# Attention and gated product on one core: x of two batches summed in DRAM, one transpose for rows 0 and 2, normalisation spread over other engines

## The chip, the core and the metric

One core of a Trainium2 chip runs the whole program. The metric is the time of one launch in microseconds (us) on the device. Of the kernel before three runs were timed: 625.11, 625.5 and 626.14 us, median 625.5 us. One more execution was profiled; all rows below come from it.

## The reference

The inputs are q, k and v (4 batches, 12 heads, 448 positions, 64 wide) and three weight matrices. What is computed, cut to what matters:

```python
scores = (q @ k.transpose(0, 1, 3, 2)) / 8          # per batch and head, 448 x 448
scores = where(mask_above_diagonal, -1e9, scores)
attn = exp(scores - max(scores)); attn = attn / (sum(attn) + 1e-9)
x = (attn @ v).transpose(0, 2, 1, 3).reshape(1792, 768)
out = ((x @ w_a) * (x @ w_b)) @ w_out               # 768 -> 1536 -> 768
```

The weights arrive as 64-bit floats and are turned into 32-bit ones on the chip.

## The kernel before, in words

The work falls into three stretches. In the **front** (to about 90 us) attention runs for batches 0 and 1, as 12 head pairs, six of each batch. In the **middle** (to about 252 us) the twelve head pairs of batches 2 and 3, called late pairs here, are threaded between the products of batches 0 and 1. After that come only products: batches 2 and 3, and parts of batches 0 and 1 in a seven-product scheme.

One head pair of attention goes like this. `scores` multiplies q and k in 64x64 tiles of TensorE (PE), two heads side by side, one row block r of 64 query positions at a time (r = 0 to 6, with 64(r+1) columns, since the mask is causal). VectorE (DVE) takes the row minimum of the negated scores (L459), ScalarE (ACT) the exponential and its sum (L465), DVE the reciprocal of the sums (L472, L474). Then each row block is normalised (L475 to L484): by GpSimd (POOL) in the front, by ACT in late pairs. `turn` transposes the normalised rows, 128 columns at a time, 16 transposes a pair (L501), into the PSUM banks t0 and t1, which ACT or DVE copy to `pt` (L299, L291). `values` multiplies with v: in the front with 128x64 tiles (L521), in late pairs with four 64x64 tiles at once (L540), row half 0 into bank `pv` and row half 1 into a bank of the ring `m`; ACT copies one, DVE adds the other, the sum is `acc`.

A front pair's x is kept as two fp32r parts, `x_hi` and `x_lo`. Later `take` (L602) builds the seven-product operands for batches 0 and 1: twelve DVE additions x_hi + x_lo into `pt` tiles, then differences and splits.

A product (L684) is three matmuls of 448 columns (hi*hi, lo*hi, hi*lo). Weights are converted on DVE with five instructions a unit (L346 to L358) and split on ACT and DVE.

What sets the order: the kernel records every operation in a `Plan`. Its `order()` plays all engines forward with costs (`dve_ns`, `act_ns`, `pool_ns`, `WAIT`) and issues the instructions in that order, so each engine's queue is fixed when the program is built, and every engine takes its queue in turn. `SLACK` holds a late pair's transposes back by that many ns in the plan; `PACE` says behind which front pair a weight unit is converted; `TAKES` at which place `take` runs. Loads and stores go through SyncE's queue (SP); DMAs that add into DRAM (L315) are issued by GpSimd.

Of the kernel before, what the change touches and what calls it, by code (L numbers as in the profile page):

```python
# [18 lines left out]
P = 128  # L19
# [12 lines left out]
PW = PO[NR]  # L32
FIRST, SECOND = ((6,), (5, 0)), ((4, 1), (3, 2))
# [3 lines left out]
NORM = ("pool", "pool", "act", "act")  # L37
TAKE = (("act", "dve"), ("act", "dve"), ("act", "act"), ("act", "act"))
# [4 lines left out]
TAKES = (15, 16, 17)  # L43
# [4 lines left out]
PACE = (0, 0, 0, 0, 0, 0, 0, 0, 1, 0, 1, 0, 0)  # L48
# [17 lines left out]
SLACK = (0, 0, 600, 600)  # L66
# [22 lines left out]
class Plan:  # L89
# [42 lines left out]
    def order(self):  # L132
# [7 lines left out]
        dge = dma = 0.0  # L140
# [9 lines left out]
        while count < n:  # L150
# [34 lines left out]
            if e == "sp":  # L185
                free[e] = at + 60.0
                dge = max(dge, at + 700.0) + 630.0
                dma = max(dma, dge) + self.ops[i][1]
                end[i] = dma + 1150.0
            elif self.ops[i][5] == "d":  # L190
                free[e] = at + 1100.0
                end[i] = free[e] + self.ops[i][1]
# [39 lines left out]
def dma_ns(nbytes):  # L232
    return nbytes / 360.0
# [3 lines left out]
def causal_attention_then_gated_product(  # L237
# [45 lines left out]
    w_m = sbuf.tile([P, 2, UW], U32, tag="w_m", name="w_m")  # L283
    w_keep = [dram.tile([P, UW], F32, name=f"w_keep{u}") for u in range(NU)]
# [28 lines left out]
    def add_up(nbytes, o, i, reads, writes):  # L313
        plan.op("pool", nbytes / 150.0 + 2500.0,
# [18 lines left out]
    def convert_unit(besides=False):  # L333
# [9 lines left out]
        def r():  # L343
# [3 lines left out]
            out=e.t, in0=high(), scalar1=0x7FF00000, scalar2=None, op0=ALU.bitwise_and), [t], [e])  # L347
        plan.op("dve", 470, lambda: nc.vector.tensor_scalar(
            out=m.t, in0=high(), scalar1=0x000FFFFF, scalar2=0x00100000,
            op0=ALU.bitwise_and, op1=ALU.bitwise_or), [t], [m])  # L350
# [74 lines left out]
    def scores(b, hp):  # L425
# [7 lines left out]
        def view(r):  # L433
            return p.t[:, PO[r]:PO[r] + D * (r + 1)]

        for part, tags in ((FIRST, ("s0", "s1")), (SECOND, ("m", "m") if b < 2 else ("t0", "t1"))):
            banks = [bank(tag, 3 if tag == "m" else 1) for tag in tags]
# [17 lines left out]
            for r in [r for rs in part for r in rs]:  # L455
# [16 lines left out]
        plan.op("dve", 200, lambda: nc.vector.tensor_scalar_add(st.t[:, rc, 0:NR], st.t[:, sm, 0:NR], 1.0e-9),  # L472
                [(st, sm, r) for r in rows], [(st, rc, r) for r in rows])
        plan.op("dve", 122, lambda: nc.vector.reciprocal(st.t[:, rc, 0:NR], st.t[:, rc, 0:NR]), [], [(st, rc, r) for r in rows])  # L474
        for r in rows:  # L475
            def norm(r=r):
                if NORM[b] == "act":
# [4 lines left out]

            ns = act_ns(D * (r + 1), False, 1) if NORM[b] == "act" else pool_ns(D * (r + 1))
            plan.op(NORM[b], ns, norm, [(st, rc, r)], [(p, r)])  # L484
# [4 lines left out]
    def turn(b, hp, n):  # L489
        p = p_of[b, hp]  # L490
        full = sb("pt", 3, [P, 2, 8, D])
        places = [(c, r) for c, o, count in groups[n] for r in range(2 * c, NR)]
        for h in range(2):
            t = bank(f"t{h}")
            some = list(enumerate(places[4 * h:4 * h + 4]))
            for part in [[x] for x in some] if b < 2 else [some]:

                def mm(part=part, t=t):
                    for i, (c, r) in part:
                        at = PO[r] + P * c - (D if b >= 2 and c == 3 else 0)  # L500
                        x = nc.tensor.matmul(  # L501
                            t.t[:, P * i:P * (i + 1)], p.t[:, at:at + P],
                            swapped if r in CROSSED else ident, is_transpose=True, start=True, stop=True,
# [3 lines left out]
                plan.op("pe", 109 * len(part), mm, [*((p, r) for _, (_, r) in part), "ident"], [t], slack=SLACK[b])  # L507
            copy(TAKE[b][h], 512, lambda full=full, h=h: full.t[:, :, 4 * h:4 * h + 4, :],
                 lambda t=t: t.t.rearrange("p (i j d) -> p j i d", i=4, j=2), [t], [(full, h)], True)
        pt[n] = full  # L510

    def values(b, hp, x):
# [3 lines left out]
        if x is not None:  # L516
# [12 lines left out]
            split_x(x, hp, lambda: ps.t[:, :S], ps, True)  # L529
            return  # L530
        more = m_bank()

        def quarters():
            for k in (0, 1, 3, 2, 5, 4, 6):
                c, row = (3, 1) if k == 6 else divmod(k, 2)
                n, o = next((n, g[1]) for n in range(2) for g in groups[n] if g[0] == c)
                o += k - 2 * c
                rows = slice(row * D, (row + 1) * D)
                for j in range(2):
                    r = nc.tensor.matmul(  # L540
                        (ps, more)[row].t[j * D:(j + 1) * D, D * k:S], vt.t[rows, c, j, :],
                        parts[n].t[rows, j, o:o + NR - k, :].rearrange("p i d -> p (i d)"), start=k < 2, stop=k in (4, 6),
# [3 lines left out]
        plan.op("pe", 15 * 107.0, quarters,  # L546
                [(vt, 0), (vt, 1), *((parts[n], h) for n in range(2) for h in range(2))], [ps, more], "q")
# [53 lines left out]

    def take(k):  # L602
        rooms = [sb("pt", 3, [P, 1024]) for _ in range(2)]
        b11, b12, b21, b22 = (((lambda t=t, i=i: t.t[:, i * S:(i + 1) * S]), (t, i)) for t in rooms for i in range(2))
        for (o, key), b, kk in ((b11, 0, k), (b12, 1, k), (b22, 1, k + 3), (b21, 0, k + 3)):
            hi, lo = xs[b]
            both(o, lambda hi=hi, kk=kk: hi.t[:, kk, :].bitcast(F32), lambda lo=lo, kk=kk: lo.t[:, kk, :].bitcast(F32), ALU.add,
                 [(hi, kk), (lo, kk)], [key])
# [502 lines left out]
```

## Time and profile before

| | us |
|---|---|
| median of the three timed runs | 625.5 |
| the profiled execution, its own time | 625.17 |
| its span, first to last instruction | 623.4 |
| PE busy in the span | 614.5 |
| DVE, ACT, POOL busy | 554.5, 390.5, 64.8 |

What lies around the span is 625.17 - 623.4 = 1.8 us. "Busy" counts the time in which at least one instruction of an engine runs; matmuls overlap each other, so a PE matmul's own duration is longer than the spacing from one to the next. A wait is idle time of an engine, put down to what ended it.

### The profile page before, as it was taken

How to read it: one execution, taken by the hardware profiler on the slowest of the kernel's cores; microseconds unless marked ns; L12 is line 12 of the kernel's file. 1: busy time of each engine (PE TensorE's matmuls, PEld its weight loads, DVE VectorE, ACT ScalarE, POOL GpSimd, SP SyncE). 2: the span in 40 equal slices, each digit the busy share in tenths (PEclk: the TensorE clock that was granted, in tenths of full speed). 3: DMA queues.
4: the chain of work that ended last, by engine and by line, in shares of the span. 5: the costliest groups of instructions: out<-in, count | busy, mean ns of one | idle time of the engine just before them, and what ended most of it. 6: DMA issues, size and time to landing. Idle time of an engine off the chain costs nothing.

```text
span 623.4 us, 11323 instructions
## 1 busy us (share of the span) xinstructions
PE 614.5 (99%) x3980; PEld 543.8 (87%) x3980; DVE 554.5 (89%) x1243; ACT 390.5 (63%) x932; POOL 64.8 (10%) x124
## 2 busy tenths in 40 slices
PE   8999999999999999999999999999999999999997
PEld 6666778888888888899999999999999999999997
DVE  7789978999999999999989997588899767889984
ACT  6989549999999999455344655344455433455530
POOL 4756320000000000000000022100000000000030
PEclk9999999999999999999999999999999999999999
DMA  8636443987686769733311668412112532112454
GB/s 277 234 116 211 157 159 109 301 269 242 248 268 243 228 244 313 261 111 102 127 52 71 214 122 201 103 52 76 52 50 97 174 110 76 53 61 83 108 90 98
DMA packets 40568, 96.02 MB, mean 154 GB/s; under 512 B 4672, under 2 KB 25152, under 8 KB 40512
## 3 DMA queue, kind: packets, MB, share of 16 engines
q1 hardware_dynamic: 37632, 90.72, 43.6%
q0 software_dynamic: 2880, 4.59, 5.3%
q8 instruction: 31, 0.51, 0.3%
q14 instruction: 25, 0.20, 0.1%
HBM read 67.37 MB, written 27.92 MB: 153 GB/s over the span
## 4 chain that ended last, share of the span: by engine, by line
PE 90%; DVE 6%; DMA 2%; ACT 1%; POOL 0%; issue 0%; SPq 0%; DVEq 0%; POOLq 0%
PE m L684 63%; PE t L684 7%; PE t L501 5%; PE s L684 3%; PE s L450 3%; DMA raw<-kT 2%; PE pv L684 2%; PE t L450 2%; PE pv L540 2%; PE m L540 1%; PE pv L521 1%; ACT early L465 1%; DVE pt L299 1%; DVE p L459 1%; PE m L450 1%; DVE early L459 1%
## 5 line engine op out<-in xcount | busy, mean ns | idle before, releaser
L684 PE MATMUL m<-x_hi,w_hi 128*128 128x448 f32 x360 | 135.1, 375 | 0.0
L684 PE MATMUL m<-x_lo,w_hi 128*128 128x448 f32 x360 | 130.5, 362 | 0.0
L684 PE MATMUL m<-x_hi,w_lo 128*128 128x448 f32 x360 | 130.3, 362 | 0.0
L291 ACT ACTIVATE w_hi<-w 128x384 fp32r<-128x384 f32 (+1 forms) x96 | 57.5, 599 | 31.1 <-PE m L684 12.0
L684 PEld LDWEIGHTS m<-x_hi,w_hi 128*128 128x128 f32 x360 | 67.8, 188 | 5.2 <-issue 0.4
L684 PEld LDWEIGHTS m<-x_hi,w_lo 128*128 128x128 f32 x360 | 67.5, 187 | 4.8
L684 PEld LDWEIGHTS m<-x_lo,w_hi 128*128 128x128 f32 x360 | 67.7, 188 | 3.6
L315 POOL DMA_DIRECT2D out<-mid x20 | 17.7, 905 | 507.1 <-ACT mid L291 497.6
L291 ACT ACTIVATE mid<-m 128x448 f32<-128x448 f32 x72 | 38.8, 541 | 45.9 <-PE m L684 38.9
L465 ACT ACTIVATE p<-p,st 128x128 f32<-128x128 f32 (+6 forms) x126 | 62.3, 499 | 8.1 <-DVE st L459 8.0
L291 ACT ACTIVATE w_hi<-w_e_s 128x384 fp32r<-128x384 f32 x72 | 37.3, 521 | 45.8 <-PE m L684 25.0
L307 DVE TENSOR_TENSOR w_lo<-w,w_hi 128x384 fp32r<-128x384 f32 (+1 forms) x96 | 62.9, 655 | 0.9 <-ACT w_hi L291 0.9
L684 PE MATMUL m<-g_hi,w_hi 128*128 128x448 f32 x144 | 53.3, 370 | 1.2 <-DVE acc L307 1.2
L307 DVE TENSOR_TENSOR w_lo<-w_e_s,w_hi 128x384 fp32r<-128x384 f32 x72 | 39.6, 550 | 14.7 <-ACT w_hi L291 13.6
L684 PE MATMUL m<-g_lo,w_hi 128*128 128x448 f32 x144 | 52.3, 363 | 0.0
L684 PE MATMUL m<-g_hi,w_lo 128*128 128x448 f32 x144 | 52.1, 362 | 0.0
L291 ACT ACTIVATE pt<-t 128x512 f32<-128x512 f32 x72 | 41.9, 594 | 10.6 <-PE t L501 10.1
L684 PE MATMUL m<-p_x,w_hi 128*128 128x448 f32 x144 | 43.4, 362 | 0.0
L291 ACT ACTIVATE g_hi<-mid 128x448 fp32r<-128x448 f32 x42 | 24.2, 575 | 19.0 <-DVE mid L307 19.0
L478 ACT ACTIVATE p<-p,st 128x64 f32<-128x64 f32 (+6 forms) x84 | 34.9, 500 | 1.1 <-DVE st L474 0.9
L355 DVE SCALAR_TENSOR_TENSOR w_e<-w,w_e 128x768 uint32<-128x768 uint32 x36 | 34.6, 960 | 0.3 <-ACT w_e L351 0.2
L353 DVE SCALAR_TENSOR_TENSOR w_m<-w_m,w 128x768 f32<-128x768 uint32 x36 | 34.3, 952 | 0.2
(178 smaller groups left out, 1471.0 us busy)
## 6 DMA issues: line engine op xcount, KB each, us to landing
w<-w SPq DMA_DIRECT2D x36, 768.0 KB, 5.9
w<-w_keep SPq DMA_DIRECT2D x48, 384.0 KB, 3.0
w_keep<-w SPq DMA_DIRECT2D x36, 384.0 KB, 5.3
raw<-qT SPq DMA_DIRECT2D x24, 224.0 KB, 4.5
raw<-kT SPq DMA_DIRECT2D x24, 224.0 KB, 4.6
v<-v SPq DMA_DIRECT2D x24, 192.0 KB, 4.3
out<-mid SPq DMA_DIRECT2D x20, 224.0 KB, 2.4
out<-mid POOLq DMA_DIRECT2D x20, 224.0 KB, 3.9
```

The lines of the kernel that those rows point to most:

```text
L291: return nc.scalar.activation(o(), i(), AF.Copy)
L307: plan.op(engine, ns, lambda: e.tensor_tensor(out=o(), in0=a(), in1=b(), op=op), reads, writes)
L315: lambda: nc.gpsimd.dma_start(out=o(), in_=i(), accum_op=ALU.add), reads, writes, "d")
L353: plan.op("dve", 869, lambda: nc.vector.scalar_tensor_tensor(out=r(), in0=m.t, scalar=2.0**32, in1=low(), op0=ALU.mult, op1=ALU.add), [m, ...
L355: plan.op("dve", 869, lambda: nc.vector.scalar_tensor_tensor(out=e.t, in0=high(), scalar=0x80000000, in1=e.t, op0=ALU.bitwise_and, op1=ALU ...
L450: x = nc.tensor.matmul(at[r][0].t[to * D:(to + 1) * D, at[r][1]], q[:, r * D:(r + 1) * D], k[:, 0:D * (r + 1)], start=True, stop=True)
L459: return nc.vector.tensor_tensor_reduce(out=view(r), in0=at[r][0].t[:, at[r][1]], in1=mask[:, S - n:], scale=-0.125, scalar=3.0e38, op0=AL ...
L465: return nc.scalar.activation(view(r), view(r), AF.Exp, bias=st.t[:, nm, r:r + 1], scale=-1.0, accum_out=st.t[:, sm, r:r + 1],)
L478: return nc.scalar.activation(view(r), view(r), AF.Copy, scale=st.t[:, rc, r:r + 1])
L501: x = nc.tensor.matmul(t.t[:, P * i:P * (i + 1)], p.t[:, at:at + P], swapped if r in CROSSED else ident, is_transpose=True, start=True, st ...
L540: r = nc.tensor.matmul((ps, more)[row].t[j * D:(j + 1) * D, D * k:S], vt.t[rows, c, j, :], parts[n].t[rows, j, o:o + NR - k, :].rearrange( ...
L684: r = nc.tensor.matmul(ps.t[:, :S], a[:, i, :], x(), start=first and n == 0, stop=last and n == 2, skip_group_check=part)
```

## The change

- **x in DRAM.** After each front pair `keep_x` stores `x_hi` to DRAM (SP) and adds `x_lo` to it with an accumulating DMA (POOL). `take` loads the sums instead of adding on DVE, and `TAKES` is (13, 15, 16), not (15, 16, 17).
- **Late pairs, transposes.** The rows of p lie close together (`LATE_PO`), rows 0 and 2 share one 128-column transpose, 15 instead of 16 a pair. Row 0's own columns now come out in row half 1 of `pt`, so `values` needs the first 64 positions of v there: a small load a pair on SP puts them into the spare end of p (`LATE_V`). The eight 64x64 steps of `values` then have 896 columns in each row half, where before it was 960 and 832. ACT now copies the `m` bank, DVE adds `pv`.
- **Normalisation.** In late pairs GpSimd does rows 3 and 6, ACT the other five. The last two front pairs are normalised by ACT, not GpSimd. The first pair's rows go to DVE (0 to 2), GpSimd (3 to 5) and ACT (6), with the reciprocal in three steps.
- **Order.** Pair 1's scores are recorded right behind pair 0's, into other banks. `PACE` is one pair later. The planner's costs change: DMA rate 340 instead of 360, accumulating DMAs, a port that DVE's bit operations and GpSimd hold in turn, `SLACK` 400 instead of 600.

```diff
-TAKES = (15, 16, 17)
+TAKES = (13, 15, 16)
...
-SLACK = (0, 0, 600, 600)
+SLACK = (0, 0, 400, 400)
...
+                if e == "pool" or self.ops[i][5] == "x":
+                    at = max(at, port)
+                    port = at + ns
...
+        if b >= 2:
+            load(D * P * 4, lambda: p.t[D:, LATE_V:LATE_V + P].rearrange("p (j d) -> p j d", j=2), lambda: v0[b, hp, 0:D, 0],
+                 [], [(p, "v")])
...
+            by = NORM0[r] if (b, hp) < (0, 1) else "pool" if r in BY_POOL and b >= 2 else NORM[b] if (b, hp) < (1, NP - LATE) else "act"
...
+                halves = [((2, 0), two(2, 2)[1]), *(two(r, 2) for r in (3, 4, 5))], [two(6, 2), *(two(r, 4) for r in (4, 5, 6))]
...
+            for row, k, n, o, count in ((1, -1, 1, 0, 1), (0, 0, 0, 0, 6), (1, 1, 0, 0, 6), (0, 2, 1, 0, 5), (1, 3, 1, 1, 4),
+                                        (0, 4, 1, 5, 3), (1, 5, 1, 6, 2), (1, 6, 0, 6, 1)):
...
-        copy("act", S, lambda: t.t, lambda: ps.t[:, :S], [ps], [t], True)
-        two_input("dve", S - D, lambda: t.t[:, D:], lambda: more.t[:, D:S], lambda: t.t[:, D:], ALU.add, [more], [t])
+        copy("act", S, lambda: t.t, lambda: more.t[:, :S], [more], [t], True)
+        two_input("dve", S - D, lambda: t.t[:, D:], lambda: ps.t[:, D:S], lambda: t.t[:, D:], ALU.add, [ps], [t])
...
+    def keep_x(b, k):
+        hi, lo = xs[b]
+        load(P * S * 4, lambda: x_first[b][k], lambda: hi.t[:, k, :].bitcast(F32), [(hi, k)], [("x1", b, k)])
+        add_up(P * S * 4, lambda: x_first[b][k], lambda: lo.t[:, k, :].bitcast(F32), [(lo, k)], [("x1", b, k)])
...
-            both(o, lambda hi=hi, kk=kk: hi.t[:, kk, :].bitcast(F32), lambda lo=lo, kk=kk: lo.t[:, kk, :].bitcast(F32), ALU.add,
-                 [(hi, kk), (lo, kk)], [key])
+            load(P * S * 4, o, lambda b=b, kk=kk: x_first[b][kk], [("x1", b, kk)], [key])
...
-            scores(*pairs[i])
+            for n in {0: (0, 1), 1: ()}.get(i, (i,)):
+                scores(*pairs[n])
```

Three places in the built programs, on the engines of which the prediction speaks. Names carry the ring's buffer number and a running number.

PE, the values of the last late pair and the first product behind them, before (pv and m are the two PSUM banks, pt the transposed rows, v the values):

```order
L684 MATMUL m0_3246<-g_hi_1320,w_lo_79 128x448
L540 MATMUL pv0_3304<-pt1_3251,v2_74 64x448 x2
L540 MATMUL m1_3307<-pt1_3251,v2_74 64x384 x2
L540 MATMUL m1_3307<-pt2_3278,v2_74 64x256 x2
L540 MATMUL pv0_3304<-pt2_3278,v2_74 64x320 x2
L540 MATMUL m1_3307<-pt2_3278,v2_74 64x128 x2
L540 MATMUL pv0_3304<-pt2_3278,v2_74 64x192 x2
L540 MATMUL m1_3307<-pt1_3251,v2_74 64x64 x2
L684 MATMUL m1_3337<-g_hi_1320,w_hi_78 128x448
```

The same place now:

```order
L731 MATMUL m1_3287<-g_hi_1362,w_lo_79 128x448
L583 MATMUL m0_3334<-pt2_3309,p1_71 64x64 x2
L583 MATMUL pv0_3337<-pt1_3285,v2_74 64x384 x2
L583 MATMUL m0_3334<-pt1_3285,v2_74 64x384 x2
L583 MATMUL pv0_3337<-pt2_3309,v2_74 64x320 x2
L583 MATMUL m0_3334<-pt2_3309,v2_74 64x256 x2
L583 MATMUL pv0_3337<-pt2_3309,v2_74 64x192 x2
L583 MATMUL m0_3334<-pt2_3309,v2_74 64x128 x2
L583 MATMUL m0_3334<-pt1_3285,v2_74 64x64 x2
L731 MATMUL m2_3361<-g_hi_1362,w_hi_78 128x448
```

Before, the next product writes the bank m1 that values has just filled; now it writes m2, and six matmuls stand ahead of the first one into m0. The two banks' column counts are 960 and 832 before, 896 and 896 now.

PE in the front, from the end of pair 0's values to the scores of pair 4 (raw0), before (t00 and t10 are the transpose banks):

```order
L521 MATMUL pv0_405<-pt0_358,v0_72 64x64 x2
L501 MATMUL t10_421<-ident_66,p1_71 128x128
L501 MATMUL t10_421<-swapped_67,p1_71 128x128
L501 MATMUL t10_421<-ident_66,p1_71 128x128 x2
L501 MATMUL t00_433<-swapped_67,p1_71 128x128 x2
L501 MATMUL t00_433<-ident_66,p1_71 128x128
L501 MATMUL t00_433<-swapped_67,p1_71 128x128
L450 MATMUL s00_441<-raw0_239 64x448 x2
```

And now:

```order
L561 MATMUL pv0_410<-pt0_363,v0_72 64x64 x2
L539 MATMUL t00_400<-swapped_67,p1_71 128x128
L539 MATMUL t10_432<-ident_66,p1_71 128x128
L539 MATMUL t10_432<-swapped_67,p1_71 128x128
L539 MATMUL t10_432<-ident_66,p1_71 128x128 x2
L469 MATMUL s00_446<-raw0_260 64x448 x2
```

Before, 8 transposes of pair 1 stand here behind 4 that went ahead of the values; now 5 stand here behind 3. Four fewer are done when pair 4's scores come up.

GpSimd in the front now, around the first of the new accumulating DMAs (early holds p of pairs 2 and 3; these rows are pair 2's last two and pair 3's first four):

```order
L506 TENSOR_SCALAR early_75<-early_75,st_69 128x384
L506 TENSOR_SCALAR early_75<-early_75,st_69 128x448
L506 TENSOR_SCALAR early_75<-early_75,st_69 128x64
L506 TENSOR_SCALAR early_75<-early_75,st_69 128x128
L326 DMA x_first0_0_81<-x_lo0_457 128x448
L506 TENSOR_SCALAR early_75<-early_75,st_69 128x192
L506 TENSOR_SCALAR early_75<-early_75,st_69 128x256
```

Before, the seven rows of pair 3 stand there without a DMA between them. Twelve such DMAs now stand in this queue, the last five in a row behind pair 9, ahead of the first late pair's rows 3 and 6.

## Rows read from the trace of the kernel before

**Rows 1.** Page, part 1: busy us, share of the span and instructions by engine

```profile
PE 614.5 (99%) x3980; PEld 543.8 (87%) x3980; DVE 554.5 (89%) x1243; ACT 390.5 (63%) x932; POOL 64.8 (10%) x124
```

**Rows 2.** PE's waits, whole span: who, for whom, total us, times, longest

```profile
PE m L684 <- DVE acc L307: 1.2, 1, 1.2
...
PE t L501 <- DVE pt L299: 1.0, 2, 0.6
PE s L450 <- DMA raw<-kT: 0.8, 2, 0.5
PE t L501 <- ACT pt L291: 0.7, 1, 0.7
PE t L501 <- POOL early L479: 0.5, 2, 0.3
```

**Rows 3.** Chain of waits: start us, us, what; late transposes, then the front

```profile
128.06 0.44 PE t L501 x4
...
11.44 8.71 DMA raw<-kT
20.29 0.99 PE s L450 x8
...
26.13 0.92 PE s L450 x8
```

**Rows 4.** Timeline of PE, end of a late pair's values: start us, us, instruction, count

```profile
123.02 0.27 PE L540 MATMUL m<-pt,v 64*64 64x64 f32 x3
...
123.16 0.34 PE L540 MATMUL pv<-pt,v 64*64 64x192 f32 x2
```

**Rows 5.** Timeline, all engines, where the last late pair's values end

```profile
250.43 0.33 PE L540 MATMUL pv<-pt,v 64*64 64x192 f32 x2
250.81 0.54 ACT L291 ACTIVATE acc<-pv 128x448 f32<-128x448 f32 x1 [1.21 <-PE pv L540]
250.82 0.62 DVE L307 TENSOR_TENSOR pt<-x_hi,x_lo 128x448 f32<-128x448 f32 x1
...
251.38 0.56 DVE L307 TENSOR_TENSOR acc<-m,acc 128x384 f32<-128x384 f32 x1
...
252.00 0.47 PE L684 MATMUL m<-g_hi,w_hi 128*128 128x448 f32 x1 [1.24 <-DVE acc L307]
```

**Rows 6.** Busy us by engine in windows (count), clock, DMA share, GB/s

```profile
12.00:20.00 8.00, 7.41 (x70) 4.95 (x70) 5.97 (x29) 8.00 (x30) 6.49 (x15) 1.00 1.01 370
...
57.00:84.00 27.00, 25.62 (x192) 19.02 (x193) 23.37 (x60) 16.36 (x46) 12.99 (x21) 1.00 0.49 163
84.00:250.00 166.00, 166.00 (x1375) 143.62 (x1377) 160.16 (x377) 152.14 (x384) 0.24 (x1) 1.00 0.71 241
```

The columns after the window's length are PE, PEld, DVE, ACT, POOL.

**Rows 7.** Timeline, GpSimd's norms in the front and one DVE instruction beside them

```profile
21.38 0.66 POOL L479 TENSOR_SCALAR early<-early,st 128x448 f32<-128x448 f32 x1
...
54.69 1.30 DVE L307 TENSOR_TENSOR w_lo<-w,w_hi 128x768 fp32r<-128x768 f32 x1
...
55.15 1.34 POOL L479 TENSOR_SCALAR p<-p,st 128x448 f32<-128x448 f32 x1
...
79.66 4.59 POOL L479 TENSOR_SCALAR early<-early,st 128x64 f32<-128x64 f32 x7 [9.97 <-DVE st L474]
```

**Rows 8.** Timeline of one late pair: reciprocal, ACT's seven norms, first transpose

```profile
121.51 0.95 DVE L307 TENSOR_TENSOR w_lo<-w,w_hi 128x768 fp32r<-128x768 f32 x1
...
125.18 0.20 DVE L474 RECIPROCAL st<-st 128x7 f32<-128x7 f32 x1
...
125.42 2.91 ACT L478 ACTIVATE p<-p,st 128x64 f32<-128x64 f32 x7
...
127.90 0.27 PE L501 MATMUL t<-swapped,p 128*128 128x128 f32 x1
```

**Rows 9.** DVE's instructions on pt, 100 to 300 us: count, ns min/median/max, from, to

```profile
L307 DVE TENSOR_TENSOR pt<-x_hi,x_lo x12: 611/615/617, 249.4 to 267.3; 128x448 f32<-128x448 f32 x12
```

**Rows 10.** Page, part 5: busy us, mean ns of one, idle before

```profile
L315 POOL DMA_DIRECT2D out<-mid x20 | 17.7, 905 | 507.1 <-ACT mid L291 497.6
```

More of the change, by code (lines that the diff above doesn't have):

```diff
@@ L283, in causal_attention_then_gated_product @@
     w_m = sbuf.tile([P, 2, UW], U32, tag="w_m", name="w_m")
+    x_first = [[dram.tile([P, S], F32, name=f"x_first{b}_{k}") for k in range(KT)] for b in range(2)]
     w_keep = [dram.tile([P, UW], F32, name=f"w_keep{u}") for u in range(NU)]
@@ L491, in turn, with two @@
         full = sb("pt", 3, [P, 2, 8, D])
-        places = [(c, r) for c, o, count in groups[n] for r in range(2 * c, NR)]
+        if b < 2:
+            places = [((r,), p.t[:, PO[r] + P * c:PO[r] + P * (c + 1)]) for c, o, count in groups[n] for r in range(2 * c, NR)]
+            halves = places[:4], places[4:]
+        else:
+            def two(r, k):
+                return (r,), p.t[:, LATE_PO[r] + D * k:LATE_PO[r] + D * (k + 2)]
+            if n == 0:
+                halves = [two(r, 0) for r in (1, 2, 3, 4)], [two(5, 0), two(6, 0), two(6, 5)]
+            else:
+                halves = [((2, 0), two(2, 2)[1]), *(two(r, 2) for r in (3, 4, 5))], [two(6, 2), *(two(r, 4) for r in (4, 5, 6))]
@@ L493, in turn @@
+        at = 0
         for h in range(2):
             t = bank(f"t{h}")
-            some = list(enumerate(places[4 * h:4 * h + 4]))
+            some = list(enumerate(halves[h]))
             for part in [[x] for x in some] if b < 2 else [some]:
                 def mm(part=part, t=t):
-                    for i, (c, r) in part:
-                        at = PO[r] + P * c - (D if b >= 2 and c == 3 else 0)
+                    for i, (rs, of) in part:
                         x = nc.tensor.matmul(
-                            t.t[:, P * i:P * (i + 1)], p.t[:, at:at + P],
-                            swapped if r in CROSSED else ident, is_transpose=True, start=True, stop=True,
-                        )
-                    return x
-                plan.op("pe", 109 * len(part), mm, [*((p, r) for _, (_, r) in part), "ident"], [t], slack=SLACK[b])
@@ L508, in turn @@
-            copy(TAKE[b][h], 512, lambda full=full, h=h: full.t[:, :, 4 * h:4 * h + 4, :],
-                 lambda t=t: t.t.rearrange("p (i j d) -> p j i d", i=4, j=2), [t], [(full, h)], True)
+                            t.t[:, P * i:P * (i + 1)], of,
+                            swapped if rs[0] in CROSSED else ident, is_transpose=True, start=True, stop=True,
+                        )
+                    return x
+                plan.op("pe", 109 * len(part), mm, [*((p, r) for _, (rs, _) in part for r in rs), "ident"], [t], slack=SLACK[b])
@@ L510, in turn @@
+            count = len(some)
+            copy(TAKE[b][h], P * count, lambda full=full, at=at, count=count: full.t[:, :, at:at + count, :],
+                 lambda t=t, count=count: t.t[:, :P * count].rearrange("p (i j d) -> p j i d", i=count, j=2), [t], [(full, h)], True)
+            at += count
         pt[n] = full
```

72 lines of the change are left out of this document (45 added, 27 removed).

## The prediction

> **What bounds the kernel now.** I read the shares of the engines first: PE is busy for 614.5 of 623.4 us, DVE for 554.5 [rows 1]. So a change gains either by taking work off PE or by removing one of PE's few waits, and a relief of another engine is worth nothing unless PE waits for it. Then PE's waits over the whole span: the five listed add up to 4.2 us, and the longest single one is 1.24 us, where a product waits for DVE's addition of the last late pair [rows 2, 5]. Of the transposes' waits (1.0, 0.7 and 0.5 us) 0.6 us lies in the start-up and 1.6 us between 57 and 84 us. The windows say where these can lie at all: from 84 to 250 us PE is busy for 166.00 of 166 us, between 57 and 84 us for 25.62 of 27 [rows 6]. In the middle only less PE work helps; in the front a better fit may.
>
> **The change part by part.** The sum is made against the profiled execution's own 625.17 us; the median of the three runs is 0.3 us above it.
>
> *One transpose less a late pair.* Four transposes take 0.44 us on the chain, 0.11 us each [rows 3]. There are 12 late pairs: 12 x 0.11 = 1.32 us off PE. It is on the path, because PE has no idle time there. The bounds are close; I take 1.32.
>
> *Values with even halves.* The columns multiplied stay the same, 1792 for each head, but the halves become 896 and 896. In the trace the row half in bank m ends at 123.02 + 0.27 = 123.29 and the one in pv at 123.16 + 0.34 = 123.50 [rows 4]: 0.21 us late for 128 columns more. Evening them takes half of that, 0.105 us a pair, 1.26 us in all. The lower end is nothing, if the added pair of 64-column steps costs as much in issue as it saves; I take 1.26, since the step sizes in between stay as they were. The small load of v that it needs, one a late pair on SP, waits for a buffer that was freed two pairs earlier; behind it in the queue stand loads of later pairs, and PE waits for no DMA in the middle.
>
> *The bank behind the last values.* Before, the next product writes m1, which DVE has yet to read: values' last matmul begins at 250.43, ACT copies pv from 250.81, DVE is in an addition on pt until it adds m at 251.38, and PE goes on at 252.00 after 1.24 us idle [rows 5]. Now the m bank is read by ACT's copy, 0.54 us in the trace, and the next product writes another bank; six matmuls stand ahead of the one that needs the copied bank. Six matmuls are longer than one copy, so the wait goes: 1.24 us. What is late next there is nothing that the trace shows: PE has no further wait to the end [rows 2]. For the other late pairs the exchange of banks is worth nothing.
>
> *x through DRAM.* Twelve additions of 0.615 us leave DVE, between 249.4 and 267.3 us [rows 9], 7.4 us. I count them at nothing: PE does not wait there, except behind the bank above. If that cover were wrong they could be worth up to 7.4 us, but no wait of PE bears it out. What comes in: 12 stores and 12 loads on SP, and 12 accumulating DMAs at 0.905 us of GpSimd each [rows 10]. An accumulating DMA waits for the store of the same tile to land, and GpSimd's norms of later pairs are queued behind it; PE's transposes wait for those. A norm of a whole pair takes 4.59 us at its slowest [rows 7]; with 0.9 us of DMA that is 5.5, and PE's period in the front is 26.13 - 20.29 = 5.84 us [rows 3]. It fits, barely in the worst pairs. The last five DMAs stand in a row ahead of the first late pair's rows 3 and 6; 4.5 us of issue, in a stretch where GpSimd has nothing else to do. Cost taken: nothing. Bounds: nothing to 2.9 us, from the longest landing of a load in the front, 8.71 us, less the period of 5.84.
>
> *The first pair on three engines, pair 1's scores earlier.* These make pair 0's transposes ready sooner. But pair 4's scores begin at 20.29 us when kT lands, 8.71 us after its issue, with the DMA engines full (1.01, 370 GB/s) [rows 3, 6]. The bytes queued ahead of it are the same now, so that landing stays at about 20.2 us, and what is won before it is waited away again. In the new order four transposes fewer stand ahead of those scores, so PE has 4 x 0.11 = 0.44 us more left to do from there on. I take a loss of 0.44; the bounds are 0.44 lost and nothing.
>
> *The front's end.* Between 57 and 84 us PE waits 0.5 us for GpSimd's norms, and 1.1 us for copies out of the transpose banks [rows 2]. The slow one is the last pair's 4.59 us [rows 7]. In the change the last two pairs' norms are ACT's, 2.91 us for seven [rows 8], and ACT has 27 - 16.36 = 10.6 us free there [rows 6], so the 0.5 goes. The 11th and 12th pairs also come sooner, with the first weight unit one pair later, so copies and conversions meet elsewhere; half of the 1.1 us is a guess. I take 1.0 of the 1.6; bounds nothing and 1.6.
>
> *Rows 3 and 6 on GpSimd.* ACT loses some 10 us of 152.14 [rows 6], which frees nothing that PE waits for. What is added is a wait of PE on GpSimd. GpSimd and DVE hinder each other: a 448-wide norm takes 0.66 us, and 1.34 with DVE's w_lo beside it, which itself takes 1.30 and not 0.95 [rows 7, 8]. In a late pair the reciprocal ends at 125.38 and the first transpose is at 127.90, 2.5 us later [rows 8]. Row 6 is now the sixth of seven in a block, 0.55 us later still. Two clear norms need at most 2 x 0.66 + 0.2 to start = 1.5 us, two held ones 2 x 1.34 + 0.2 = 2.9, against 3.05: no wait, even with `SLACK` 0.2 us less, or at most a tenth or two. DVE itself: 24 norms x 0.35 us = 8.4 us in a stretch where it has 166 - 160.16 = 5.8 us free [rows 6]; if every norm meets such an instruction, 2.6 us reach PE. I take none, as only some of the front's norms are lengthened, and keep 2.6 as the bound.
>
> Here the Trainium skill speaks against the change. The page SBUF — State Buffer, section Who interferes with whom, says that DVE and GpSimd share a port pair as an exclusive lock, that a DVE instruction with two inputs in SBUF contends with a GpSimd instruction that reads SBUF, and that the loser is blocked for the whole instruction. The trace's 1.34 against 0.66 us agrees in kind; by the rule the hold would reach w_lo's whole 0.95 us, not 0.68, and the two norms would end 0.4 us past their transposes, some 4 us in 12 pairs; rival (c) works a hold of that length out from rows.
>
> *The sum.* 1.32 + 1.26 + 1.24 + 1.0 - 0.44 = 4.4 us. 625.17 - 4.4 = 620.8; for the median, a little above its profiled run, 621.0 us.
>
> **The rivals.**
> (a) *Only what is certain.* The even halves bring nothing and the front's waits come back in other places: 621.0 + 1.26 + 1.0 = 623.3 us. For it: the front's waits hang on meetings of engines that the new order deals anew. Against it: the 0.21 us by which one half ends late is plain.
> (b) *GpSimd's queue in the front.* An accumulating DMA that waits for a store in the busy first 25 us holds a pair's norms, PE waits once for 2.9 us, and the 1.0 us of the front isn't won: 621.0 + 2.9 + 1.0 = 624.9 us, no change that counts. For it: the landing of 8.71 us. Against it: the first such DMA belongs to pair 0 and stands among pair 3's rows, which PE comes to only after the values of pairs 1 and 2.
> (c) *Slower: PE waits for GpSimd in every late pair.* DVE is busy nearly throughout, so both norms are held for 0.95 us each and the reciprocal comes 0.7 us later, as DVE pays 0.35 twice: 0.2 + 2 x 0.66 + 2 x 0.95 + 0.7 = 4.1 us against 3.05, a wait of 1.05 us a pair, 12.6 us: 633.6 us. It decides from 4.4 / 12 = 0.37 us a pair on. For it: DVE has 5.8 us to spare in 166. Against it: most norms in the front are not held twice.
>
> **How the numbers follow.** Forecast 0.69, (a) 0.15, (b) 0.09, (c) 0.07. A change of 0.2%, 1.25 us, is about what a measurement of this kernel can tell from none. Faster by more: the forecast and (a), 0.84. Within: most of (b), 0.08. Slower: (c) and the rest of (b), 0.08. The range for 8 in 10: down to 618.8 us, if the other 0.6 us of the front's waits go, the start costs nothing and the time that PE needs to refill after a wait, which its busy time hides, comes on top (about 1 us); up to 624.0, which takes in (a) and the 2.6 us of DVE's bound, and leaves out (b) and (c).
>
> **What would show it.** PE's instructions: 372 transposes, not 384; in a late pair's values the two banks' last matmuls end together, and from the first to the next instruction is 0.1 us shorter. No wait on DVE's acc near 250 us, no POOL wait near 80 us. Pair 4's scores still begin at about 20.3 us, behind a DMA. It is wrong if PE's waits list transposes behind GpSimd between 84 and 250 us (rival c), if PE waits in the front for norms with an accumulating DMA ahead of them on GpSimd (b), or if pair 4's scores begin well before 20 us, since then the start is worth something.

## The result: 621.4 us, and the profile after

The changed kernel takes 621.40 us (median of six runs, 619.97 to 621.79), the kernel before 626.17 us in the same minutes (625.11 to 628.22): the ratio is 0.9919, with a 95% interval of 0.9901 to 0.9937. The forecast was 621.0 us, in a range of 618.8 to 624.0. The profiled execution of the changed kernel took 621.33 us (span 619.6), that of before 625.17 (span 623.4). The latter lies 1.0 us under its median, so the two profiles differ by only 3.84 us where the medians differ by 4.8.

Part 1 of the page (busy us, share of the span, instructions), for [rows 1]:

```profile
PE 610.7 (99%) x4012; PEld 542.4 (88%) x4012; DVE 552.0 (89%) x1238; ACT 381.6 (62%) x923; POOL 85.8 (14%) x142
```

PE has 3.8 us less to do, about what the spans differ by: the kernel is as full as before, with less in it. PE's waits over the whole span (us in total, times, longest), for [rows 2]:

```profile
PE s L469 <- DVE x_lo L318: 1.4, 1, 1.4
PE fill L1096 <- DVE warm L1075: 1.1, 1, 1.1
PE t L469 <- DMA raw<-kT: 0.9, 1, 0.9
PE t L539 <- DVE p L501: 0.8, 1, 0.8
PE t L539 <- POOL p L506: 0.5, 2, 0.3
```

All of them lie ahead of 66 us. The 1.24 us behind the last late pair's values [rows 5] are gone: the last values end, and the product follows.

```profile
244.33 0.28 PE L583 MATMUL m<-pt,v 64*64 64x64 f32 x4
244.54 0.48 PE L731 MATMUL m<-g_hi,w_hi 128*128 128x448 f32 x1
```

Two new waits stand in the start, in PE's timeline: the first transposes of pair 0 wait for DVE's norms, and pair 4's scores begin at 20.70 us (20.29 before, [rows 3]). That wait is put down to a DVE instruction; the load of this pair's kT, issued at 10.85 us, landed at 20.57.

```profile
10.94 0.30 PE L539 MATMUL t<-swapped,p 128*128 128x128 f32 x1 [0.79 <-DVE p L501]
...
20.70 0.66 PE L469 MATMUL s<-raw 64*64 64x448 f32 x4 [1.37 <-DVE x_lo L318]
```

Busy us by engine in two of the windows of [rows 6] (PE, PEld, DVE, ACT, POOL with counts; then clock, DMA share, GB/s):

```profile
57.00:84.00 27.00, 26.51 (x217) 19.97 (x216) 24.88 (x61) 23.48 (x64) 8.02 (x12) 1.00 0.90 232
84.00:250.00 166.00, 166.00 (x1430) 145.10 (x1429) 163.10 (x382) 139.59 (x361) 24.94 (x26) 1.00 0.79 262
```

PE is as full between 84 and 250 us as before and gets through 1430 instructions in place of 1375. ACT has 12.5 us less to do, GpSimd 24.7 more.

Three marks in PE's timeline split the run: the start of the first late pair's scores, of the 781st of the products' 2376 matmuls (just behind the taking of x), and of the last of them. The stretch up to the first mark is called the front below, that between the first two the middle (it runs on past 252 us, to take in the taking of x).

| profiled execution | first late scores | 781st product matmul | middle | last product matmul |
|---|---|---|---|---|
| before | 91.74 | 300.24 | 208.50 | 619.52 |
| changed | 91.91 | 296.31 | 204.40 | 615.45 |

So the front gave nothing in these two profiles (0.17 us lost), the middle gave 4.10 us, and from the second mark to the last product both take the same within 0.14 us.

### The profile page after: what moved, and what is told of

It is laid out like the page before. It is cut to its first block, busy times and chain, and to the rows that moved or that the text cites. A ratio compares the mean times of both kernels' runs of the same rounds, so it can differ in the third digit from the quotient of the medians.

```text
span 619.6 us, 11515 instructions
## 1 busy us (share of the span) xinstructions
PE 610.7 (99%) x4012; PEld 542.4 (88%) x4012; DVE 552.0 (89%) x1238; ACT 381.6 (62%) x923; POOL 85.8 (14%) x142
## 4 chain that ended last, share of the span: by engine, by line
PE 94%; DVE 3%; DMA 1%; ACT 1%; POOL 1%; issue 0%
PE m L731 65%; PE t L731 7%; PE t L539 6%; PE s L731 3%; PE s L469 3%; PE pv L561 2%; PE pv L731 2%; PE t L469 2%; PE m L583 2%; PE pv L583 1%; DVE p L478 1%; DMA x_first<-x_hi 1%; POOL p L506 1%; ACT p L484 1%; DVE pt L310 1%; PE m L469 1%
## 5 line engine op out<-in xcount | busy, mean ns | idle before, releaser
L731 PE MATMUL m<-x_hi,w_hi 128*128 128x448 f32 x360 | 133.7, 371 | 0.0
L484 ACT ACTIVATE p<-p,st 128x448 f32<-128x448 f32 (+6 forms) x126 | 62.5, 498 | 10.3 <-DVE st L478 10.2
L506 POOL TENSOR_SCALAR p<-p,st 128x256 f32<-128x256 f32 (+6 forms) x62 | 42.9, 765 | 128.9 <-ACT p L484 52.0
L302 ACT ACTIVATE pt<-t 128x512 f32<-128x512 f32 x72 | 38.7, 575 | 5.8 <-PE t L539 5.8
L369 DVE SCALAR_TENSOR_TENSOR w<-w_m,w_e 128x768 f32<-128x768 f32 x36 | 35.6, 989 | 0.1
```

The costliest lines, as they stand in the source:

```text
L302: return nc.scalar.activation(o(), i(), AF.Copy)
L369: plan.op("dve", 869, lambda: nc.vector.scalar_tensor_tensor(out=wt.t, in0=r(), scalar=2.0**-52, in1=e.t.bitcast(F32), op0=ALU.mult, op1=A ...
L484: return nc.scalar.activation(view(r), view(r), AF.Exp, bias=st.t[:, nm, r:r + 1], scale=-1.0, accum_out=st.t[:, sm, r:r + 1],)
L506: return nc.gpsimd.tensor_scalar(out=view(r), in0=view(r), scalar1=st.t[:, rc, r:r + 1], scalar2=1.0, op0=ALU.mult, op1=ALU.mult)
L731: r = nc.tensor.matmul(ps.t[:, :S], a[:, i, :], x(), start=first and n == 0, stop=last and n == 2, skip_group_check=part)
```

## The experiments

Times are medians; "before" is the kernel before in the same minutes. The ratio is taken over the single executions, so it is not the quotient of the two medians. Front and middle are read from the one profiled execution of each kernel (before: 91.74 and 208.50; changed: 91.91 and 204.40).

| run | us | before | ratio (95%) | front | middle |
|---|---|---|---|---|---|
| sharing alone | 626.95 | 626.01 | 1.0008 (0.9996 to 1.0020) | 92.01 | 209.71 |
| banks back | 620.50 | 626.01 | 0.9906 (0.9888 to 0.9923) | 90.33 | 204.40 |
| x on DVE | 621.74 | 626.01 | 0.9939 (0.9916 to 0.9961) | 90.65 | 208.43 |
| weights late | 623.93 | 626.01 | 0.9967 (0.9953 to 0.9980) | 91.98 | 208.13 |
| ACT's norms | 627.17 | 626.40 | 1.0010 (0.9996 to 1.0023) | 91.14 | 210.47 |
| sharing + norms | 622.45 | 626.40 | 0.9937 (0.9916 to 0.9959) | 91.11 | 205.62 |
| norms alone | 623.73 | 626.40 | 0.9955 (0.9937 to 0.9972) | 91.15 | 207.23 |
| changed, again | 621.19 | 626.40 | 0.9910 (0.9890 to 0.9930) | 91.98 | 204.40 |
| old start | 620.19 | 625.66 | 0.9902 (0.9880 to 0.9925) | 90.39 | 205.06 |
| one row on GpSimd | 622.43 | 625.66 | 0.9940 (0.9918 to 0.9962) | 90.43 | 206.48 |
| three rows on GpSimd | 626.68 | 625.66 | 1.0016 (1.0000 to 1.0033) | 91.85 | 209.32 |
| old start, banks back | 619.62 | 626.31 | 0.9896 (0.9881 to 0.9911) | 90.22 | 204.43 |

The two columns on the right help where medians lie close. The middle is the same 204.40 us in three profiles (both of the changed kernel, and the banks back). The front is not so steady: both profiles of the changed kernel, the banks back, ACT's norms, one row and three rows have the same instructions in the same order there, and take 90.33 to 91.98 us. So a front from a single profile does not tell a microsecond.

**The sharing alone.** The kernel before with `LATE_PO`, the pairing and the even halves:

```diff
+LATE_PO = (320, 0, 128, 1152, 384, 1408, 704)
+                halves = [((2, 0), two(2, 2)[1]), *(two(r, 2) for r in (3, 4, 5))], ...
```

> The kernel before with the sharing of the transpose alone: LATE_PO, 15 transposes for a late pair, even halves of the values, the small load of v; x is still taken on DVE, norms, planner's numbers, order of the start and roles of the two banks are those of before. Theory: the gain lies in work that PE no longer has, 12 x 0.11 us of transposes and 12 x 0.07 us of values (1.579 to 1.508 us from first to last in the two traces), 2.2 us in all; the 1.24 us behind the last values stay. So 2.2 us faster than before, ratio 0.9965, and 372 transposes. Rival: the gain needs the relief of DVE and ACT (x through DRAM, rows 3 and 6 on GpSimd), since with one transpose less the copies and exponentials become the late ones: then PE waits between 84 and 250 us and under 1 us is won, ratio above 0.9985.

It gained nothing, so the theory fell. PE's waits between 84 and 275 us:

```profile
PE m L706 <- ACT mid L293: 1.3, 2, 0.8
PE t L518 <- ACT pt L293: 0.6, 1, 0.6
```

PE has less to do, and waits for ACT instead: three waits between 209 and 236 us, where the kernel before has none. The middle is 1.2 us longer than before. The work that was taken off PE is real, but PE wasn't the only engine that had little time to spare: ACT is busy for 148.76 of the 166 us from 84 to 250.

**ACT's norms.** The changed kernel without its smallest part:

```diff
-BY_POOL = (6, 3)
+BY_POOL = ()
```

> The changed kernel with ACT normalising all rows of the late pairs again; the rest is the change's. As predicted, rows 3 and 6 on GpSimd were worth nothing, so 621.4 us, the changed kernel's within 0.3. The rival theory, formed on the run with the sharing alone, which gained nothing: the relief of ACT (139.6 us of 166 in place of some 150) and the earlier norms are what the gain rests on. In the order PE turns from products to transposes 40 times in the late pairs here, and 24 times in the changed kernel. Then PE waits for copies or norms between 84 and 250 us, 2 to 4 us with the refilling behind them, and the time is 623 to 625.5 us, ratio to the kernel before 0.996 to 1.000.

The prediction's zero is refuted: without this part nothing of the change's gain is left. What happens is seen in three views. The window of the late pairs:

```profile
84.00:250.00 166.00, 166.00 (x1410) 143.10 (x1412) 160.10 (x378) 150.89 (x384) 1.72 (x2) 1.00 0.77 258
```

PE is busy for all of it, so no wait gives anything away. But the late pairs come on more slowly. The last pair's values begin here, in PE's timeline:

```profile
249.15 0.27 PE L583 MATMUL m<-pt,p 64*64 64x64 f32 x2
```

In the changed kernel that was at 242.87, and from the first late pair's values to the last's a pair takes 12.88 us on average, not 12.35 (12.81 before). PE fills the time with products: 549 of their matmuls are done when the last values begin, against 522. Then they run short. The taking of x comes late, because its loads go into `pt` rooms, the tiles that hold the transposed rows until values has read them: four of these loads are issued from 251.00 us on, 244.72 in the changed kernel, and land 7 us after their issue. DVE waits 4.74 us for the next of them, issued at 260.18 and landed at 268.48:

```profile
268.50 0.63 DVE L318 TENSOR_TENSOR pt<-pt,pt 128x448 f32<-128x448 f32 x1 [4.74 <-DMA pt<-x_first]
```

and PE waits between 250 and 290 us for what comes out of it:

```profile
PE m L731 <- DVE acc L318: 1.9, 1, 1.9
PE m L731 <- ACT mid L302: 0.7, 1, 0.7
PE m L731 <- DVE w_lo L318: 0.4, 1, 0.4
PE m L731 <- DVE p_x L318: 0.3, 1, 0.3
```

These are 3.2 us that the changed kernel doesn't have. The rest of the 6.1 us by which the middle is longer is 2.9 us more of PE's time outside waits. Refilling behind the waits and the order (PE turns from products to transposes 40 times, not 24) are the likely causes; the runs don't part them.

**Norms alone, and norms with the sharing.** The kernel before with

```diff
+BY_POOL = (6, 3)
-SLACK = (0, 0, 600, 600)
+SLACK = (0, 0, 400, 400)
```

(and the planner's rule for the port), without and with the sharing.

> The kernel before with rows 3 and 6 of the late pairs on GpSimd alone (planner's allowance and port rule as in the change), 16 transposes a pair, no sharing. By the prediction the norms are worth nothing by themselves: 626.0 us, ratio 1.000 within 0.001. If the relief of ACT alone is what the gain rests on: 622 to 624, ratio below 0.997. If GpSimd's norms come late for the transposes (rival c): above 1.002, with PE's waits behind GpSimd. PE turns to transposes 44 times here, against 39 before.

> The kernel before with two parts of the change: the shared transpose (with the even halves) and rows 3 and 6 of the late pairs on GpSimd, with the planner's allowance for transposes and its rule for the shared port as in the change. x is taken on DVE, the start and the roles of the two banks are those of before. Rival theory (both parts together carry the middle): PE turns to transposes 26 times, has no wait between 84 and 250 us, and the late pairs are 2.7 us shorter (1.31 transposes, 1.07 values, 0.34 fewer turns), so 623.3 us with the wait behind the last values, 621.9 without it: ratio 0.9935 to 0.996. If x through DRAM or the other order of the start is needed too, the ratio is above 0.998.

Norms alone are 2.7 us faster than before, sharing alone is 0.9 slower (its interval takes in no change), both are 3.95 faster: with the norms the sharing is worth about 1.3 us by the medians, whose intervals overlap, and 1.6 in the middle; without them nothing. The planner's numbers go with the norms in these runs; they were not tried apart. In the profile of norms alone PE has no wait between 84 us and the end: the one of 1.24 us is gone, though the banks have their old roles and DVE still adds up x. That wait is all that the middle wins by the norms alone (207.23 us, 208.50 before). The rest of the 2.7 isn't found there; the front, whose order is another too, is 0.6 us shorter in the profile, less than fronts differ among themselves. With both parts one wait is left, at 271.04 us:

```profile
PE m L711 <- ACT mid L297: 0.9, 1, 0.9
```

**One row, three rows on GpSimd.**

```diff
-BY_POOL = (6, 3)
+BY_POOL = (6,)            # and (6, 5, 3)
```

> The changed kernel with row 6 alone of the late pairs normalised by GpSimd, row 3 on ACT. With both rows on GpSimd it takes 621.2 to 621.4 us, with none 627.2. Theory: what the GpSimd norms are worth is the time that ACT gets back, since ACT feeds PE's products and is next behind PE as the bound; row 6 gives back the longer half of it, so the time lies between the two, 623 to 625 us, with PE's waits for ACT's or DVE's results at 255 to 285 us, of 1 to 2 us. Rival: it is not ACT's time but the number of PE's turns from products to transposes (24 with both, 40 with none, 31 here): then PE has no wait there and the time follows the turns, 621.4 + 7 x 0.09 = 622.0.

> The changed kernel with rows 6, 5 and 3 of the late pairs on GpSimd. If ACT's time were still short with two rows, a third would gain: below 620.9 us. Theory: with two rows PE has no wait between 70 us and the end, so ACT's time is no longer what ends last; a third is worth nothing, 621.4 within 0.3, or costs something where GpSimd's three norms, 0.77 us each in the mean and up to 1.34, end behind their transposes. By rival (c) of the prediction, held norms 2 x 1.34 against 3.05 us from reciprocal to the last rows' transposes: three are 4.0 us and PE would wait up to 1 us in some of the 12 pairs, up to 633 us if in all.

One row brings 4.7 of the 6 us by the medians, 4.0 if each is set against the kernel before in its own minutes, and 4.0 of the 6.1 us in the middle, 66%. PE's late waits are only 0.5 us, less than the theory of ACT's time had. But ACT's busy time from 84 to 250 us is 150.89, 143.69 and 139.59 us with no, one and two rows, so one row brings 64% of that relief; of the turns it saves 9 of 16 (40, 31, 24). Both fit the 66%, and the run doesn't part them. What goes with the times is how fast the pairs come: 12.88, 12.52 and 12.35 us a pair.

With three rows the sign turns (12.84 us a pair, with ACT at 133.38 us), and rival (c)'s mechanism is there. PE's waits between 84 and 250 us:

```profile
PE t L539 <- POOL p L506: 3.0, 5, 1.0
```

GpSimd's norms in this stretch, by form, with three rows (busy us, mean ns of one):

```profile
L506 POOL TENSOR_SCALAR p<-p,st 128x448 f32<-128x448 f32 x12 | 15.5, 1292 | 0.0
L506 POOL TENSOR_SCALAR p<-p,st 128x384 f32<-128x384 f32 x12 | 15.4, 1283 | 0.0
L506 POOL TENSOR_SCALAR p<-p,st 128x256 f32<-128x256 f32 x12 | 8.0, 667 | 104.6 <-ACT p L484 47.3 <-DVE st L494 46.6 <-DVE st L478 10.7
```

and in the changed kernel:

```profile
L506 POOL TENSOR_SCALAR p<-p,st 128x448 f32<-128x448 f32 x12 | 14.4, 1200 | 0.0
L506 POOL TENSOR_SCALAR p<-p,st 128x256 f32<-128x256 f32 x12 | 9.3, 777 | 115.3 <-ACT p L484 52.0 <-DVE st L494 30.6 <-DVE st L478 23.6
```

Three rows need 1.29 + 1.28 + 0.67 = 3.2 us in the mean, over the 3.05 us that the prediction had from the reciprocal to the last rows' transposes; two need 1.20 + 0.78 = 2.0 us in the mean and are clear of it.

**The banks back.** The changed kernel with

```diff
-                        (ps, more)[row].t[j * D:(j + 1) * D, at:at + count * D], v,
+                        (more, ps)[row].t[j * D:(j + 1) * D, at:at + count * D], v,
```

and ACT copying pv, DVE adding m, as before.

> The changed kernel with the roles of the two banks of a late pair's values as before: row half 0 in bank m, half 1 in pv, ACT copies pv and DVE adds m. Theory: the product after the last late pair's values waits for DVE again, 1.2 us, so 622.6 us, ratio to the changed kernel 1.002. Rival: the wait went because DVE no longer has the additions of x in its queue there, not because of the exchange; then PE still has no wait near 247 us, the time is the changed kernel's within 0.3 us.

The rival holds: with the old roles there is no wait there either, and the middle is the changed kernel's to 0.01 us. The median is 0.7 to 0.9 us below the changed kernel's two, which the intervals don't part; in the profiles that difference lies in the front. The product follows the values at once:

```profile
242.75 0.28 PE L583 MATMUL pv<-pt,v 64*64 64x64 f32 x4
242.97 0.48 PE L731 MATMUL m<-g_hi,w_hi 128*128 128x448 f32 x1
```

**x on DVE.** The changed kernel without `keep_x`; the sums are made in `take`, at the places of before:

```diff
-TAKES = (13, 15, 16)
+TAKES = (15, 16, 17)
...
-            load(P * S * 4, o, lambda b=b, kk=kk: x_first[b][kk], [("x1", b, kk)], [key])
+            both(o, lambda hi=hi, kk=kk: hi.t[:, kk, :].bitcast(F32), lambda lo=lo, kk=kk: ..., ALU.add, ...)
```

> The changed kernel without x through DRAM: no stores and accumulating DMAs of x in the front, the twelve additions of 0.6 us are back on DVE in takes at 15, 16 and 17. Theory: the 7.4 us of DVE were hidden, and so were the DMAs; the time is the changed kernel's within 0.3 us, 621.4, and PE has no new wait over 0.3 us. Rival 1: the sums in DRAM carry a part of the gain (DVE is busy for 163 of 166 us in the late pairs' stretch, and the taking of x runs beside them): slower by up to 7.4 us, with PE's waits behind DVE between 230 and 260 us. Rival 2: the accumulating DMAs hurt the front: the waits of 0.2 us at 65 and 66 us go and the time is 0.5 us shorter.

The median, 621.74, is the changed kernel's within 0.5 us, and five of the seven runs took 621.1 to 622.4. The profiled one is one of two longer ones, 624.45: its first late pair's scores came at 90.65 us, 1.3 us sooner than in the changed kernel, and then PE waited 2.22 us for ACT at 270 us. Behind that wait products start 0.37 us apart, not 0.20:

```profile
270.25 0.37 PE L732 MATMUL m<-x_hi,w_lo 128*128 128x448 f32 x1
272.84 0.74 PE L732 MATMUL m<-x_hi,w_hi 128*128 128x448 f32 x1 [2.22 <-ACT mid L302]
273.38 0.57 PE L732 MATMUL m<-x_lo,w_hi 128*128 128x448 f32 x1
273.75 0.57 PE L732 MATMUL m<-x_hi,w_lo 128*128 128x448 f32 x1
```

The window 274 to 276 us shows a granted clock of 0.50 of full speed, 1.2 in place of 2.4 GHz:

```profile
274.00:276.00 2.00, 2.00 (x7) 1.74 (x7) 2.00 (x5) 0.29 (x1) 0.00 (x0) 0.50 0.59 183
```

So where DVE adds up x and the other parts are there, PE waits behind the taking of x (0.94 us with norms and sharing alone, 2.22 here); with x through DRAM and two rows on GpSimd no profile shows a wait for ACT there. That x through DRAM pays for it in the front is not shown, as 90.65 us lies among the fronts of the programs that have it. In the median the run without it is 0.3 to 0.6 us longer, which the intervals don't part.

**Weights late.** The three weight loads of `START` go to turns 2, 3 and 4 of the loop over the pairs:

```diff
-START = (("q", 0), ..., ("v", 1), ("w", 0), ("v", 2), ("w", 1), ("w", 2))
+START = (("q", 0), ..., ("v", 1), ("v", 2))
```

> The changed kernel with the three weight loads of the start issued behind the raw rows of pairs 6, 7 and 8 (one a pair), not among the first ten loads. Theory: pair 4's scores begin when their kT lands, and that is set by the bytes queued ahead of it, so the landing comes sooner and the wait of 1.37 us before 20.70 us goes; pair 4's scores begin at about 19.3 us and the whole kernel is up to 1.4 us shorter, 620.0, ratio to the changed kernel 0.998. Rival: the landing is not set by the bytes ahead, or the next pairs' loads or the weights' conversions come late in its place: PE waits as much somewhere between 12 and 60 us, the first late pair's scores still begin at about 91.9 us and the time stays within 0.3 us of 621.4, or grows.

The rival holds, and more. Pair 4's kT lands 1.0 us sooner than in the changed kernel's first profile, at 19.57 us; but with the weight loads in their old place it landed anywhere from 19.55 to 20.72 us, so this isn't shown to be their doing. The scores begin at 20.78 without a wait: PE now has its other work ahead of them. It waits 1.22 us for a copy at 59.01 and 0.53 for `w_lo` at 63.92, and the first late scores come at 91.98. What was put off is missed at 255.75 us, where PE waits 1.87 us for `w_lo` and the clock falls as above (0.50 in the window 260 to 262): 2.5 us lost by the medians.

**The old start.** The changed kernel with pair 0's reciprocal in one piece, its norms all on GpSimd, and pair 1's scores in their old place.

```diff
-        for lo, hi in PHASES if (b, hp) < (0, 1) else ((0, NR),):
+        for lo, hi in ((0, NR),):
```

> The changed kernel with the start of before: pair 0's reciprocal in one piece, its seven rows normalised by GpSimd, pair 1's scores in their old place and banks; the rest is the change's. The prediction took 0.44 us off the change's gain for its start, so this would give 621.0 us. The theory now: in the changed kernel PE waits 0.8 us for pair 0's norms at 10.2 us, 1.5 us in the second run of it, and there the granted clock was 0.50 in the stretch 14 to 16 us; the old start has no such wait, pair 4's scores begin at 20.3 us as before, and the time is 0.5 to 1 us shorter, 620.4 to 620.9, ratio to the kernel before 0.990. Rival: pair 0's early transposes are worth something behind 20 us: then it is slower than 621.4 by some tenths.

> The changed kernel itself once more, so that it is timed on the same chip and in the same minutes as the three others: 621.4 us within 0.5, ratio to the kernel before 0.992.

620.19 us, against 621.19 and 621.40 of the changed kernel: 1.0 to 1.2 us less, or 0.3 to 0.7 if each is set against the kernel before in its own minutes, and the intervals overlap. The profiles point to the start without proving its price. PE's waits up to the first late scores are 1.4 us with the old start (those over 0.1, without the first for `warm`), 3.8 in the first profile of the changed kernel, and these scores come at 90.39, not 91.91. But programs with the new start reached them at 90.33 and 90.43 too. What all six profiles with the changed kernel's front have is a wait for pair 0's norms, of 0.8 to 1.5 us, which the old start doesn't have. It was longest in the second profile of the changed kernel, and there the clock was 0.50 behind it:

```profile
11.76 0.30 PE L539 MATMUL t<-swapped,p 128*128 128x128 f32 x1 [1.50 <-DVE p L501]
```

```profile
14.00:16.00 2.00, 2.00 (x20) 1.36 (x18) 1.66 (x9) 2.00 (x7) 0.27 (x1) 0.50 1.02 417
```

A last kernel joins the old start with the old roles of the banks, since with the new roles and the old start PE waited 0.37 us for ACT's copy behind the last values.

> The changed kernel with the start of before (as in the run of the old start) and the banks' roles of before (as in the run of the banks): ACT copies pv, DVE adds m. With the old start alone PE waits 0.37 us for ACT's copy behind the last late pair's values; with the banks of before alone PE had no wait there. If the exchange of banks only trades one reader for another, this wait goes and the time is 619.2 to 620.2 us, ratio to the kernel before 0.988 to 0.990. If DVE is late there in this order, a wait behind DVE's addition takes its place, 0.4 to 1.2 us, and it is no better than 620.2.

619.62 us, the lowest median of all, 0.6 us under the old start alone, which the intervals don't part. Its profile has no such wait, and its middle is 204.43 us, 0.63 less; PE has no wait over 0.1 us from 17 us to the end.

## Why the prediction was right in its number and not in all its steps

*The transposes* (1.32 us). PE runs 372 transposes, and in the middle the transposes and products take 1.65 us less together (from each start to the next, waits left out). That takes in 12 x 0.11, and the fewer turns, 24 and not 39. The size fits. But "it is on the path, because PE has no idle time there" was half the condition: with the sharing alone none of it arrived.

*The even halves* (1.26 us, bounds nothing and 1.26). Before, a late pair's values and the scores behind them take 2.48 us up to the next product:

```profile
121.70 0.54 PE L540 MATMUL pv<-pt,v 64*64 64x448 f32 x1
...
124.18 0.47 PE L684 MATMUL m<-x_hi,w_hi 128*128 128x448 f32 x1
```

In the changed kernel they take 2.40:

```profile
119.28 0.48 PE L583 MATMUL pv<-pt,v 64*64 64x384 f32 x1
...
121.67 0.47 PE L731 MATMUL m<-x_hi,w_hi 128*128 128x448 f32 x1
```

Where a product follows the values at once it is 1.64, not 1.72. So 0.08 us a pair came, not 0.105, about 1.0 us in all: right in kind, a quarter too large. (The end is taken at the product because before, the first scores start while values still runs. The expectation of the sharing alone had 0.07, with 1.579 us for before, which the trace doesn't bear out.)

*The bank* (1.24 us). The wait is gone, for another reason than given. With the old roles it is gone as well, and in the kernel with the norms alone too, where DVE still adds up x. The wait was a meeting of the last values with one long job of DVE; in every other order that was run this wait for DVE is gone, and the exchange of roles by itself is worth nothing (204.40 us in the middle with either). "Six matmuls are longer than one copy" was no safety either: with the old start PE waited 0.37 us for just this copy.

*The start* (0.44 us lost, bounds 0.44 and nothing) and *the front* (1.0 us won). Together 0.56 us won, measured 0.17 lost in the two profiles. The front's size holds: between 57 and 84 us PE is idle for 0.49 us, not 1.38. Which edit does it was not tried apart; with the norms alone, where GpSimd still normalises the last front pairs, the idle time there is gone too, and 1.4 us of other waits stand at 52 and 53 us. The start is the term that was mis-sized. The wait of pair 0's transposes for DVE, 0.8 to 1.5 us in those six, was not in the sum. The landing at about 20.2 us was right (19.55 to 20.72 with this start), and the wait for it is nothing in some profiles and 1.37 us in another. The six profiles with the changed kernel's front reach the first late scores at 91.27 us in the mean, the two with the old start at 90.31: some 1.0 us in place of 0.44, but with 1.65 from the first to the last of the six, so the size stays open.

*x through DRAM* (nothing, bounds 0 to 2.9 lost). The median of the run without it differs by 0.3 to 0.6 us from the changed kernel's: neither a gain nor a loss that counts. One reading behind this term is wrong. GpSimd's slowest seven norms before are not those of 4.59 us:

```profile
64.26 5.43 POOL L479 TENSOR_SCALAR early<-early,st 128x64 f32<-128x64 f32 x7 [1.38 <-ACT pt L291]
```

With 0.9 us of DMA that is 6.3, over the period of 5.84: by its own figures it didn't fit.

*Rows 3 and 6 on GpSimd* (nothing; "frees nothing that PE waits for"). This step failed, and it was the largest: without it the change is 627.17 us, no gain at all. The sentence was true of the trace of before, where PE never waits for ACT in the middle. It doesn't hold once PE's work shrinks: the late pairs then come only as fast as ACT delivers their exponentials, norms and copies (12.88 us a pair without this part, 12.35 with it), and the pairs' pace settles when the `pt` rooms are free and x can be taken. Whether it is ACT's busy time that counts or the shorter way from the reciprocal to the transposes when two engines share the norms, the runs don't part. The sum came out right because its other terms already assumed that the middle stays free of waits, which is what this part buys; and because the front's 0.7 us too much and the middle's 0.3 too little stand against each other. The number is in part luck.

The price of GpSimd's norms was right in the mean, not at its bound. The Trainium skill (SBUF — State Buffer, section Who interferes with whom) says that whichever of the two engines issues first has the shared port for its whole instruction and the other blocks. The trace agrees in kind: of the twelve norms of 448 columns four are clear (0.63 to 0.64 us), five take 1.32 to 1.34 and three 1.72 to 1.74. The mean is 1.20, 0.54 over the 0.66 of a clear one [rows 7]; a hold of `w_lo`'s whole 0.95 us [rows 8] in each is not what it shows. The three longest are over the 1.34 that the prediction took as the most, and the longest two of one pair take 1.37 + 1.72 = 3.1 us, 3.3 with the 0.2 to start, where it had 2.9 at most against 3.05. PE still has no wait for GpSimd behind 66 us.

*The rivals.* (a) came true in the front, which gave nothing, and for a fifth of the halves. (b) came in small, in one of the two profiles of the changed kernel: PE waits 0.5 us for GpSimd in the front, at 65 us, for norms that stand behind an accumulating DMA, and that DMA had waited for its store. The prediction named this as a sign that it is wrong; the price is a sixth of the 2.9 us.

```profile
61.32 0.88 POOL L326 DMA_DIRECT2D x_first<-x_lo  x1 [1.10 <-DMA x_first<-x_hi]
61.94 3.91 POOL L506 TENSOR_SCALAR p<-p,st 128x128 f32<-128x128 f32 x6
```

(c) did not come with two rows, and came with three: 3.0 us of PE's waits for GpSimd in the late pairs.

## What to carry to other kernels

An engine that is 91% busy next to one that is 100% busy isn't free: before work is taken off the first engine, ask what the second still has to deliver in the shorter time, and price the two edits together, since the first alone may give nothing (here the sharing). "PE never waits for it" values a relief only at PE's present speed. Where the full engine fills its time with other ready work (here 549 products' matmuls in place of 522 by the last pair's values), the waits come only when that work runs out, here more than 20 us later.

## What was not expected of the hardware

A wait of PE of 1.4 to 2.2 us was followed by a granted clock of 0.50 (1.2 GHz) in four places: at 14 us in two profiles, at 260 and at 274 us. Products then start 0.373 us apart, not 0.20; nine of them at 260 us cost 1.6 us, almost as much as the wait of 1.87 itself. Other waits as long were followed by no such fall (1.37 and 1.42 us in the start, 1.89 us at 280 us), so the trace alone doesn't say when it comes.
